# Two of q's five weight blocks as seven-product blocks, with their forms stored in DRAM by the k stage, and the split of M moved to the last stage

## The chip, the cores and the metric

One core of one Trainium2 chip. The metric is device time in microseconds (us) of one launch, the median of several runs; lower is better. One more execution is recorded by the hardware profiler, and it has a time of its own.

## The reference

`S = 2048` tokens, `D = 640`, `F = 1536`, 32 heads of 20 channels, all in f32:

```python
q, k, v = split(x @ wqkv)                       # (heads, S, 20) each
phi = lambda t: where(t > 0, t + 1, exp(t)) + 1e-6
kv  = einsum("hsd,hse->hde", phi(k), v);  z = phi(k).sum(s)
a   = (phi(q) @ kv) / (phi(q) . z + 1e-6) @ wo
b   = (sigmoid(x @ w_gate) * (x @ w_up)) @ w_down
g   = sigmoid((x * gate_w).sum(-1))
out = g * a + (1 - g) * b
```

## The kernel before

**Tiles and products.** The tokens lie in four groups of 512, taken as two pairs; pair 1 goes first, pair 0 second. Everything is transposed: weights are the stationary operand in blocks of 128 columns, the tokens of a group stream as 512 columns. For precision each f32 operand is split into a high and a low part (`split`, L219: ScalarE rounds the high part, VectorE subtracts for the low part), and each product is three passes, high·high, high·low, low·high (`mm3`, L189; its three calls are L190 to L192). "A product" in this text is one such pass.

**Stages.** The k stage (0 to 144.7 us) computes k and phi(k) for all tokens and `gt` = xᵀ·phi(k). Then come, for each pair, a q phase (`q_phase`, L1503) and an f stage (`f_phase`, L1530: gate, up and down weights, with the GLU). After the f stage of pair 0 the products of M with phi(q) end the kernel. In the q phase of pair 1 the small matrix M is made between the units: `kv_part(hg)` (L1168) multiplies a slice of `gt` with a slice of wv for six heads (the last slice has two) and keeps the block diagonal (`kvt`, then `kvh` and `kvl`), `m_part(hg)` (L1185) multiplies that with the slice of wo, and both store their results: `ms` high and low go to `mh_dram` and `ml_dram`. `m_rows` (L1317), in pair 1's f stage, reorders them into `mp_dram` with eight DRAM-to-DRAM transfers. `z_part` (L1144) follows the last unit.

**Plain units and blocks.** q's 640 columns are five blocks u of 128 columns. A plain unit `q_unit(pr, u, b, b12)` (L1011) is one block for one of the pair's two groups: five k tiles, three passes each, 15 products of 512 columns; in pair 0 two of the five tiles of group b = 1 come in halves of 256 columns. Two blocks for two groups are four units, 60 products. The f stage uses `Block` (L957) instead, which makes the four results of two weight columns times two groups in seven products of submatrices (`s1` to `s7`, a Strassen-like scheme) of 6, 9, 6, 9, 6, 9 and 9 passes, 54 in all. It needs sums of weights (`wsum`, split into `wu` of 384 columns and `ws` of 1152) and sums of tokens (`xst`, split into `xth` and `xtl`), besides the split columns themselves (`wg`). In pair 1 the weight forms are made on the spot and stored to `w_dram` (`store_w`, L793); in pair 0 they are loaded from there (`load_form`, L862). `wg` is 640 KB, `wu` 384 KB, `ws` 1152 KB, high and low parts together.

**phi.** `phi_q` (L1003) takes a product's bank through two ScalarE operations (`qe`, `qr`) and one VectorE operation into `qr`, and stores it to `p_dram` from POOL's queue. `qe` and `qr` come from a ring of four tiles.

**What sets the order.** Each engine executes its instructions in program order, and the program writes that order out by a small planner (`Order`, L47 to L158): it keeps an estimated clock for TensorE, ScalarE and VectorE; queued items (splits, sums, each with its two costs and perhaps a time from which its load is expected) are put in between the products when they fit (`_fits`: their end may be up to a slack behind TensorE's clock), or when a product needs them (`need`). `items` go ahead of `lazy`. Loads are issued by SP's queue, stores by POOL's.

Of the kernel before, what the change touches and what calls it, by code (L numbers as in the profile page):

```python
# [15 lines left out]
P = 128  # L16
# [4 lines left out]
TG = 512  # L21
# [24 lines left out]
class Order:  # L46
# [6 lines left out]
    def __init__(self):  # L53
        self.slack(False)
        self.pe = self.act = self.vec = 0.0
        self.items, self.lazy = [], []
        self.busy = False
        self.parts = self.pend = None
# [5 lines left out]
    def add(self, a, v, fn, key=None, ready=None, lazy=False, first=False):  # L64
        q = self.lazy if lazy else self.items
        q.insert(0 if first else len(q), (a, v, fn, key, ready))

    def then(self, fn):

        if self.parts is None:  # L70
            fn()
        else:
            self.parts.append(fn)

# [18 lines left out]
    def _fits(self, q):  # L93
        if not q:
            return False
        a, v, fn, key, ready = q[0]
        if ready is not None and self.pe < ready():
            return False
        end_a = self.act + a
        end = max(self.vec, end_a if a else 0.0) + v  # L100
        return not ((a and end_a > self.pe + self.slack_a) or (v and end > self.pe + self.slack_v))

    def fill(self):
        if self.busy:
            return
        while True:
            for q in (self.items, self.lazy):
                if self._fits(q):
                    self._run(q.pop(0))
                    break  # L110
            else:
                if self.pend and max(self.vec, self.pend[2]) + self.pend[3] <= self.pe + self.slack_v:
                    self._flush()
                return
# [11 lines left out]
    def need(self, key, now=True):  # L126
        for q in (self.items, self.lazy):
# [40 lines left out]
def gated_mix_kernel(ctx: ExitStack, tc: tile.TileContext, xt, xn, wk, wv, wo, wst_q, wst_f, out_t):  # L168
# [79 lines left out]
    w_dram = {}  # L248
    m_dram = [dram.tile([D, D], F32, name=n) for n in ("mh_dram", "ml_dram")]
# [143 lines left out]


# [70 lines left out]
    def queue_ks():  # L465
        for s, sums in ((1, (0, 2, 1)), (0, ()), (2, ()), (3, (3,))):
            for j in range(2):
                for t in sums:
                    order.add(0, v_cost(HW), lambda t=t, j=j: k_sum(t, j))
            for j in range(2):  # L470
                order.add(a_cost(HW), v_cost(HW), lambda s=s, j=j: k_form(s, j), ("ks", s))
        order.add(a_cost(HW), 2 * v_cost(HW), k_fifth_d, ("ks", 5))

# [254 lines left out]
    for c in range(1, 4):  # L728
        ck = chunks[c]
        if c == 1:  # L730
            a, b = KPlain(2), KPlain(3)
            order.need((ck, "plain"))
            queue_ks()
            queue_xn(2)
            for k in range(KC):
                a.k(k)
                order.fill()
            a.phi_a()
            for k in range(KC):
                b.k(k)  # L740
                order.fill()
                if k == 0:
                    a.phi_b()
                    order.add(0, 0.6, constants)
            order.need(("ks", 5))
            for t in range(2):
                k_split(tok(2, t))
        else:
            a, b = KBlock(2 * c), KBlock(2 * c + 1)
            for n in range(1, 6):  # L750
                order.need((ck, n))
                if c == 2 and n >= 3:
                    order.need(("ks", (1, 0, 2)[n - 3]))
                getattr(a, f"s{n}")()
                getattr(b, f"s{n}")()
                if n == 2:
                    queue_xn(2 * c)
# [12 lines left out]
            b.s6()  # L770
            a.phi_b()
            order.need(("pk", 2 * c - 1))
            k_split(tok(2 * c, 0))
            b.s7()
            b.sum_b()
            k_split(tok(2 * c, 1))
        if c == 3:
# [15 lines left out]
            def store_w(n, i):  # L793

                w_dram[n[2], i] = dram.tile(list(WT[n, i].shape), F32, name=f"w{n[2]}{i}")
                nc.gpsimd.dma_start(w_dram[n[2], i], f32(WT[n, i]))
# [38 lines left out]
    for u in range(4, 10):  # L835
        glast.part(u, 0, 2, tags[u], out=False)
        order.fill()
        if u == 5:
            for n in range(2):
                wg_split(("q", 1, n), w_stage[n])  # L840
    p1_tail = [lambda u=u: glast.out(u) for u in range(4, 10)]
    p1_cm.__exit__(None, None, None)
# [19 lines left out]
    def load_form(n, i):  # L862
        t = (wg_tile, wu_tile, ws_tile)[i]()
        nc.sync.dma_start(f32(t), w_dram[n[2], i])
        put(n, i, t)


    entries = [("q", 1, u) for u in (0, 2, 4)] + [("f", 1, f) for f in range(FC)]
# [20 lines left out]
    def queue_q(pr, u):  # L889
# [4 lines left out]
        def fn():  # L894
            if pr:
                wg_split(m, WST[n][:, u % 2])
                if u % 2 or u == KC - 1:
                    order.then(load_w)
# [5 lines left out]
    def queue_g(n):  # L904

        order.add(a_cost(D), v_cost(D), lambda: wg_split(n, WST[n][:, 0]), ("wg", n), lambda: W_AT.get(n, 1e9),
                  first=n[2] > 1)
# [231 lines left out]
    def z_perm():  # L1139
        zperm = f32(ws_tile())[:, 0, :D]  # L1140
# [27 lines left out]
    def kv_part(hg):  # L1168
        c0, w = hg_slice(hg)
        v = MV[hg]  # L1170
        ps = ps_tile("ch")
        for m in range(KC):
# [8 lines left out]
        order.add(0, v_cost(bdn), lambda: vec2(kvl[:w, :w], kvt[:w, :w], f32(kvh[:w, :w]), OP.subtract), ("kv", hg),  # L1181
                  first=True)
        load_mv(hg + 2)

    def m_part(hg):  # L1185
# [15 lines left out]
    load_mv(1)  # L1201
    load_mo(0)
# [6 lines left out]
    d_loads = entries[3:] + [("q", 0, u) for u in range(KC)]  # L1209
# [107 lines left out]
    def m_rows():  # L1317

        for m in range(2):
            for d in range(4):  # L1320
                nc.gpsimd.dma_start(mp_dram[d * H:(d + 1) * H, :, m],
                                    m_dram[m].rearrange("(h u d) n -> d h u n", u=KC, d=4)[d])
# [180 lines left out]
    def q_phase(pr, b12, extra):  # L1503

        units = [(u, b) for u in range(KC) for b in range(2)]
# [3 lines left out]
        for j, (u, b) in enumerate(units):  # L1509
            order.need((nx[1], "plain" if b else 2))  # L1510
            q_unit(pr, u, b, b12)
            if b and u + 2 < KC:
                queue_q(pr, u + 2)
                if not pr:
                    order.need(("wg", ("q", pr, u + 2)), False)
            elif b and not pr:
                load_form(("f", 0, u + 2 - KC), 0)
            elif b and u + 2 == KC:
                queue_g(("f", pr, 0))
                queue_s(("f", pr, 0))  # L1520
            for fn in extra.get(j, ()):
                fn()
            order.fill()
        order.slack(False)
# [5 lines left out]
    def f_phase(pr, hooks={}):  # L1530
# [4 lines left out]
        def step(f, s):  # L1535
# [14 lines left out]
            after_f(f, blk, s)  # L1550
# [18 lines left out]

        step(0, 1)  # L1570
        step(0, 2)
        for f in range(FC):
# [3 lines left out]
            if not pr and f % 2 and f > 1:  # L1576
                if f == FC - 1:
                    load_m(0)
# [54 lines left out]
    extra = {j: [] for j in range(10)}  # L1633
    extra[1] += [lambda: queue_wo(1), lambda: queue_wo(0)]
    for hg in range(NHG):
        extra[hg + 3].append(lambda hg=hg: m_part(hg))
    for hg in range(NHG):
        extra[hg + 1].append(lambda hg=hg: kv_part(hg))
    extra[7].append(z_perm)
    extra[9] += [z_part, m_close]  # L1640
    q_phase(1, lambda k: [(b12h[:, k], b12l[:, k])], extra)
# [12 lines left out]
    def load_forms(f, *forms):  # L1654
        for i in forms:
            load_form(("f", 0, f), i)

    tail = f_phase(1, {
        (3, 7): [m_rows],
        (6, 7): [lambda: other[0].load()],  # L1660
        (FC - 2, 7): [lambda: load_forms(0, 1, 2)],
        (FC - 1, 2): [lambda: queue_a(0, 2), lambda: queue_a(2, 4)],
        (FC - 1, 6): [lambda: queue_a(4, 5, 2)],
        (FC - 1, 7): [lambda: load_forms(1, 1, 2), queue_b],
# [6 lines left out]
    nx[0].queue_sums()  # L1671
    nx[1].queue_sums()
# [3 lines left out]
    q_phase(0, lambda k: [(c_h[c][:, k], c_l[c][:, k]) for c in range(2)], {  # L1676
# [92 lines left out]
    tail = f_phase(0, {  # L1769
# [83 lines left out]
```

## Time and profile before

| | us |
|---|---|
| runs | 754.95, 755.49, 755.50 |
| median | 755.49 |
| profiled execution | 755.98 |
| its span in the trace | 754.3 |
| TensorE busy | 747.2 (99%) |
| VectorE busy | 547.4 (73%) |
| ScalarE busy | 308.6 (41%) |
| GpSimd (POOL) busy | 89.1 (12%) |
| q phase of pair 1 | 144.69 to 191.28 |
| f stage of pair 1 | to 421.89 |
| q phase of pair 0 | 421.89 to 456.37 |

A row of the timeline has the start, the duration, engine, line, operation, output and inputs, shape, and in brackets how long the engine was idle before it and what ended that. Matmuls overlap, so the distance between their starts, not their duration, is what each costs. A row of a window has the stretch, its length, the busy time of TensorE, weight loads, VectorE, ScalarE and GpSimd with the instruction counts, the granted clock of TensorE, the DMA share and GB/s. A row of TensorE's waits has who waited for whom, the total in us, how often, and the longest. A row of a group has the count, then busy us and mean ns, then the idle time ahead of it and what ended it. A row of DMA issues has the count, KB each and median us from issue to landing.

### The profile page before, as it was taken

How to read it: one execution, taken by the hardware profiler on the slowest of the kernel's cores; microseconds unless marked ns; L12 is line 12 of the kernel's file. 1: busy time of each engine (PE TensorE's matmuls, PEld its weight loads, DVE VectorE, ACT ScalarE, POOL GpSimd, SP SyncE). 2: the span in 40 equal slices, each digit the busy share in tenths (PEclk: the TensorE clock that was granted, in tenths of full speed). 3: DMA queues.
4: the chain of work that ended last, by engine and by line, in shares of the span. 5: the costliest groups of instructions: out<-in, count | busy, mean ns of one | idle time of the engine just before them, and what ended most of it. 6: DMA issues, size and time to landing. Idle time of an engine off the chain costs nothing.

```text
span 754.3 us, 10042 instructions
## 1 busy us (share of the span) xinstructions
PE 747.2 (99%) x3696; PEld 641.1 (85%) x3696; DVE 547.4 (73%) x963; ACT 308.6 (41%) x578; POOL 89.1 (12%) x146
## 2 busy tenths in 40 slices
PE   9999999999999999999999999999999999999998
PEld 7999999988888888888888888888888888887886
DVE  4877575887676678877788864575868776886864
ACT  5664537266555534343344444253323223212110
POOL 0210111023222322112121210000000000000000
PEclk9999999999999999999999999999999999999999
DMA  8553537787887797776475744965454546277333
GB/s 260 122 160 71 140 63 185 191 275 247 312 316 271 262 386 286 266 271 226 181 261 221 297 164 154 356 244 206 158 227 150 225 137 244 91 267 254 114 134 117
DMA packets 60518, 160.51 MB, mean 213 GB/s; under 512 B 9575, under 2 KB 23399, under 8 KB 57269
## 3 DMA queue, kind: packets, MB, share of 16 engines
q1 hardware_dynamic: 44933, 99.15, 39.3%
q0 software_dynamic: 15392, 60.56, 22.9%
q8 instruction: 29, 0.48, 0.3%
q14 instruction: 20, 0.16, 0.1%
q10 hardware_dynamic: 144, 0.16, 0.1%
HBM read 97.33 MB, written 60.56 MB: 209 GB/s over the span
## 4 chain that ended last, share of the span: by engine, by line
PE 80%; DMA 3%; DVE 1%; ACT 1%; SPq 0%; issue 0%
PE dd L190 8%; PE dd L192 8%; PE dd L191 8%; PE ch L190 7%; PE ch L191 7%; PE ch L192 7%; PE rot L191 6%; PE rot L190 6%; PE rot L192 6%; PE cc L190 5%; PE cc L191 5%; PE cc L192 5%; DMA pden<-p_dram 2%; DMA wv_sb<-wv 1%; PE ch L1173 1%; DMA xnst<-xn 1%
## 5 line engine op out<-in xcount | busy, mean ns | idle before, releaser
L202 ACT ACTIVATE c<-ch 128x512 f32<-128x512 f32 x72 | 43.0, 597 | 161.7 <-PE ch L192 159.9
L206 DVE TENSOR_TENSOR hf<-c,hf 128x512 fp32r<-128x512 f32 x63 | 43.2, 688 | 28.0 <-ACT hf L202 27.7
L206 DVE TENSOR_TENSOR tb<-dd,tb 128x512 f32<-128x512 f32 x75 | 51.1, 688 | 14.2 <-PE dd L192 13.9
L206 DVE TENSOR_TENSOR c<-cc,c 128x512 f32<-128x512 f32 x48 | 32.9, 685 | 30.3 <-ACT c L202 23.4
L202 ACT ACTIVATE c<-c 128x512 f32<-128x512 f32 x48 | 30.2, 628 | 49.7 <-DVE c L206 49.7
L206 DVE TENSOR_TENSOR tb<-rot,tb 128x512 f32<-128x512 f32 x64 | 43.5, 687 | 6.0 <-PE rot L192 5.7
L202 ACT ACTIVATE hf<-c 128x512 fp32r<-128x512 f32 x63 | 39.3, 625 | 18.2 <-DVE c L206 17.3
L190 PE MATMUL dd<-xrh,wg 128*128 128x512 f32 x102 | 40.0, 392 | 0.0
L192 PE MATMUL dd<-xrh,wg 128*128 128x512 f32 x102 | 39.8, 390 | 0.0
L191 PE MATMUL dd<-xrl,wg 128*128 128x512 f32 x102 | 39.8, 390 | 0.0
L190 PE MATMUL ch<-xth,ws 128*128 128x512 f32 x96 | 37.3, 389 | 0.0
L191 PE MATMUL ch<-xtl,ws 128*128 128x512 f32 x96 | 37.3, 389 | 0.0
L192 PE MATMUL ch<-xth,ws 128*128 128x512 f32 x96 | 37.3, 389 | 0.0
L191 PE MATMUL rot<-pkl,xnh 128*128 128x320 f32 x102 | 31.7, 311 | 1.0 <-DVE pkl L210 0.6
L190 PE MATMUL rot<-pkh,xnh 128*128 128x320 f32 x102 | 31.5, 309 | 0.0
L192 PE MATMUL rot<-pkh,xnl 128*128 128x320 f32 x102 | 31.4, 308 | 0.0
L206 DVE TENSOR_TENSOR c<-c,c 128x512 f32<-128x512 f32 x44 | 30.2, 686 | 1.3 <-ACT c L202 0.9
L190 PE MATMUL cc<-xbh,ws 128*128 128x512 f32 x72 | 28.0, 389 | 0.0
L191 PE MATMUL cc<-xbl,ws 128*128 128x512 f32 x72 | 28.0, 389 | 0.0
L192 PE MATMUL cc<-xbh,ws 128*128 128x512 f32 x72 | 28.0, 389 | 0.0
L202 ACT ACTIVATE pq<-pl 128x512 fp32r<-128x512 f32 x14 | 8.5, 631 | 39.0 <-DVE pl L210 39.0
L1103 POOL DMA_DIRECT2D om_dram<-om x4 | 2.2, 540 | 186.9 <-ACT om L202 186.9
(473 smaller groups left out, 2309.3 us busy)
## 6 DMA issues: line engine op xcount, KB each, us to landing
w<-ws POOLq DMA_DIRECT2D x12, 1152.0 KB, 6.6
ws<-w SPq DMA_DIRECT2D x12, 1152.0 KB, 7.8
wst<-wst_f SPq DMA_DIRECT2D x12, 640.0 KB, 4.8
w<-wg POOLq DMA_DIRECT2D x12, 640.0 KB, 5.0
wd<-wd POOLq DMA_DIRECT2D x12, 640.0 KB, 6.5
wg<-w SPq DMA_DIRECT2D x12, 640.0 KB, 4.1
xst<-xt SPq DMA_DIRECT2D x10, 640.0 KB, 7.0
wf<-wd SPq DMA_DIRECT2D x10, 640.0 KB, 5.7
```

The lines of the kernel that those rows point to most:

```text
L190: nc.tensor.matmul(out, l_hi, r_hi, start=first, stop=False, skip_group_check=True)
L191: nc.tensor.matmul(out, l_hi, r_lo, start=False, stop=False, skip_group_check=True)
L192: nc.tensor.matmul(out, l_lo, r_hi, start=False, stop=last, skip_group_check=True)
L202: nc.scalar.activation(out, src, fn, **kw)
L206: nc.vector.tensor_tensor(out, a, b, op=op)
L1103: nc.gpsimd.dma_start(om_dram[:, g], om)
L1173: nc.tensor.matmul(ps[:w, :w], v[:, m, :w], gt[:, m, c0:c0 + w], start=(m == 0), stop=(m == KC - 1))
```

## The change

- q's blocks u = 2 and 3 go through `Block(("q", pr, 2))` in both pairs; blocks 0, 1 and 4 stay plain units (`Q_PLAIN`). In pair 1 the block's products s1 to s7 follow the last units; kv parts and M parts stand between them, the last ones on the bank pair `rot`. In pair 0 `q_phase` is a generator whose last products s5 to s7 alternate with the first products of the f stage's first block, whose sigmoid is held until after its s3.
- The weight forms of blocks 2 and 3 are made in the k stage by a new `queue_qw(2)`, as lazy items: one load, ten splits, five sums and ten stores to `w_dram["q", 2, i]`; both q phases load them back.
- `m_part` stores M in f32 as it is (`m_dram`), `m_rows` reorders it with four transfers into `mr_dram`, and a new `queue_m` loads it in five pieces in the f stage of pair 0, splits each and stores it to `mp_dram`. These are in a new queue `spare`, behind `lazy`.
- The wv slices have three buffers instead of two. `z_perm` uses a tile of pool `m1`.
- `Order` has queues `urgent` (any item of it that fits may go), `spare` and `soon`: `follow` puts a VectorE step (phi's last, `kvl`) off until the clock of VectorE has come to the point where ScalarE is done.
- In pair 0 `queue_both` takes the sums and splits of both halves of the tokens in turns.
- The f stage's first forms in pair 1 are queued earlier in the q phase (`queue_s` after block 1, `queue_g` after block 4).

```diff
+    def queue_qw(u):
+        raw = qs.tile([P, 2, D], F32, name="qraw", tag="qraw")
+        nc.sync.dma_start(raw, wst_q[:, u:u + 2])
+        at = max(order.pe, order.vec) + 5.0
...
+            def fn():
+                t = qs.tile([P, 2, w], F32R, name="qp", tag="qp", bufs=3)
+                split(t[:, 0, :n], t[:, 1, :n], src)
+                order.then(lambda: nc.gpsimd.dma_start(w_dram["q", u, i][:, :, c:c + n], f32(t[:, :, :n])))
...
-    def phi_q(g, u, src):
+    def phi_q(g, u, src, after="p"):
         e, r = tt("qe"), tt("qr")
-        act(e, src, AF.Exp, "p")
+        act(e, src, AF.Exp, after)
         act(r, src, AF.Relu)
-        vec3(r, e, 1.0, r, OP.min, OP.add, "a")
-        nc.gpsimd.dma_start(p_dram[:, u, g], r)
+        def rest():
+            vec3(r, e, 1.0, r, OP.min, OP.add)
+            nc.gpsimd.dma_start(p_dram[:, u, g], r)
+        order.need("phi")
+        order.follow(v_cost(TG), rest, "phi")
...
-            v = mp.tile([P, KC, bdn], F32, name="wv_sb", tag="wv_sb", bufs=2)
+            v = mp.tile([P, KC, bdn], F32, name="wv_sb", tag="wv_sb", bufs=3)
...
-        ms = [m1_tile(t, "ms", F32R, bdn) for t in ("ma", "mb")]
+        ms = m1_tile(("ma", "mb")[hg % 2], "ms", F32, bdn)
         for h in range(2):
-            ps = ps_tile("cc")
+            ps = ps_tile(tag)
             cs = slice(h * HALF, (h + 1) * HALF)
             mm3(ps[:w, :HALF], kvh[:w, :w], kvl[:w, :w], woh[:w, cs], wol[:w, cs], True, True)
-            split(ms[0][:w, cs], ms[1][:w, cs], ps[:w, :HALF], "p")
-        for m, dst in zip(ms, m_dram):
-            nc.gpsimd.dma_start(dst[c0:c0 + w], f32(m[:w]))
+            act(ms[:w, cs], ps[:w, :HALF], AF.Copy, "p")
+        nc.gpsimd.dma_start(m_dram[c0:c0 + w], ms[:w])
...
+    def queue_m(u=0):
+        raw = down_pool[1].tile([P, D], F32, name="mr", tag="mr")
+        nc.sync.dma_start(raw, mr_dram[:, u])
...
+            t = down_pool[1].tile([P, 2, D], F32R, name="mt", tag="mt")
+            split(t[:, 0], t[:, 1], raw)
+            def rest():
+                nc.gpsimd.dma_start(mp_dram[:, u], f32(t))
+                if u + 1 < KC:
+                    queue_m(u + 1)
+            order.then(rest)
+        order.add(a_cost(D), v_cost(D), fn, "m", lambda: at, spare=True)
...
     def q_phase(pr, b12, extra):
-        units = [(u, b) for u in range(KC) for b in range(2)]
+        units = [(u, b) for u in Q_PLAIN for b in range(2)]
+        n = ("q", pr, 2)
...
+        blk = Block(n)
+        for s in range(1, 8):
+            if s > 1:
+                order.need((nx[0] if pr else nx[1], s if s < 7 else 2))
+            getattr(blk, f"s{s}")()
+            if s == 3:
+                phi_q(2 * pr, 2, blk.c11, "v")
+            elif s == 6:
+                phi_q(2 * pr + 1, 3, blk.c22, "v")
+                phi_q(2 * pr, 3, blk.ch)
+            elif s == 7 and pr:
+                phi_q(2 * pr + 1, 2, blk.c12, "v")
...
+            for fn in extra.get(j + s, ()):
+                fn()
+            order.fill()
+            if not pr and s > 4:
+                yield
```

More of the change, by code (lines that the diff above doesn't have):

```diff
@@ L73, in then, with follow, follow_up @@
             self.parts.append(fn)
+    def follow(self, v, fn, key=None):
+        self.soon.append((self.act, v, fn, key))
+    def follow_up(self, n=1):
+        for at, v, fn, key in self.soon[:n]:
+            self.soon.pop(0)
+            was, self.busy = self.busy, True
+            self.vec = max(self.vec, at)
+            fn()
+            self.busy = was
     def _flush(self):
@@ L247, in gated_mix_kernel @@
     om_dram = dram.tile([P, NG, TG], F32, name="om_dram")
-    w_dram = {}
-    m_dram = [dram.tile([D, D], F32, name=n) for n in ("mh_dram", "ml_dram")]
+    m_dram = dram.tile([D, D], F32, name="m_dram")
+    mr_dram = dram.tile([P, KC, D], F32, name="mr_dram")
     bdn = HPG * DH
@@ L392, in queue_forms, with queue_both @@
         nx[0].queue_sums()
+    def queue_both(nx):
+        w = 2 * CW
+        for n, t, k in ((0, 1, 3), (0, 0, 4), (0, 2, 5), (3, 3, 6)):
+            for c in nx:
+                for m in {(0, 1): (0, 1, 2), (3, 3): (3,)}.get((n, t), ()):
+                    order.add(0, v_cost(w), lambda c=c, m=m: c.sum(m), None, lambda c=c: c.at)
+            for c in nx:
+                order.add(a_cost(w), v_cost(w), lambda c=c, t=t: c.form(t), (nx[1], k) if c is nx[1] else None)
     pa_cm = tc.tile_pool(name="pa", bufs=1, side="right")
@@ L840, in gated_mix_kernel @@
                 wg_split(("q", 1, n), w_stage[n])
+    order.need("qw")
     p1_tail = [lambda u=u: glast.out(u) for u in range(4, 10)]
+    qs_cm.__exit__(None, None, None)
     p1_cm.__exit__(None, None, None)
@@ L863, in load_form @@
         t = (wg_tile, wu_tile, ws_tile)[i]()
[L864 removed]
+        nc.sync.dma_start(f32(t), w_dram[n[::2] + (i,)])
         put(n, i, t)
[L868 removed]
+    Q_PLAIN = (0, 1, 4)
+    entries = [("q", 1, u) for u in (0, 4)] + [("f", 1, f) for f in range(FC)]
     WST, WS, W_AT = {}, {}, {}
@@ L1180, in kv_part, with m_part @@
         KV[hg] = (kvh, kvl)
[L1181 to L1185, printed above, removed]
+        order.follow(v_cost(bdn), lambda: vec2(kvl[:w, :w], kvt[:w, :w], f32(kvh[:w, :w]), OP.subtract), ("kv", hg))
+        load_mv(hg + 3)
+    def m_part(hg, tag="cc"):
         c0, w = hg_slice(hg)
@@ L1201, in gated_mix_kernel @@
     load_mv(1)
+    load_mv(2)
     load_mo(0)
@@ L1208, in gated_mix_kernel @@
     wd_dram = {}
-    d_loads = entries[3:] + [("q", 0, u) for u in range(KC)]
+    d_loads = entries[2:] + [("q", 0, u) for u in Q_PLAIN]
     tb = None
@@ L1317, in m_rows, with fn @@
     def m_rows():
[L1319 to L1322, printed above, removed]
+        for d in range(4):
+            nc.gpsimd.dma_start(mr_dram[d * H:(d + 1) * H], m_dram.rearrange("(h u d) n -> d h u n", u=KC, d=4)[d])
+    def queue_m(u=0):
+        raw = down_pool[1].tile([P, D], F32, name="mr", tag="mr")
+        nc.sync.dma_start(raw, mr_dram[:, u])
+        at = max(order.pe, order.vec) + 9.0
+        def fn():
+            t = down_pool[1].tile([P, 2, D], F32R, name="mt", tag="mt")
[6 more added lines that the diff above has]
+        order.add(a_cost(D), v_cost(D), fn, "m", lambda: at, spare=True)
     def m_close():
@@ L1511, in q_phase @@
             q_unit(pr, u, b, b12)
[L1512 to L1520, printed above, removed]
+            if b:
+                if u == 0:
+                    queue_q(pr, 4)
+                    if not pr:
+                        order.need(("wg", ("q", pr, 4)), False)
+                elif u == 1:
+                    load_form(n, 0)
+                    if pr:
+                        queue_s(("f", pr, 0))
+                elif pr:
+                    load_form(n, 1)
+                    load_w()
+                    queue_g(("f", pr, 0))
+                else:
+                    load_form(("f", 0, 0), 0)
+            elif pr and u == 4:
+                load_form(n, 2)
             for fn in extra.get(j, ()):
@@ L1549, in step @@
                 tails[f - 1][s]()
-            after_f(f, blk, s)
+            if s == 3 and f == 0 and not pr:
+                for _ in q:
+                    pass
+                after_f(f, blk, 2)
+            elif s != 2 or f or pr:
+                after_f(f, blk, s)
             if s == 7:
@@ L1577, in f_phase @@
                 if f == FC - 1:
+                    while any(it[3] == "m" for it in order.spare) or order.pend:
+                        order.need("m")
+                        order._flush()
                     load_m(0)
@@ L1632, in gated_mix_kernel @@
         fn()
-    extra = {j: [] for j in range(10)}
+    extra = {j: [] for j in range(13)}
     extra[1] += [lambda: queue_wo(1), lambda: queue_wo(0)]
[L1635 to L1641, printed above, removed]
+    for hg, j in enumerate((3, 4, 5, 7, 8, 10)):
+        extra[j].append(lambda hg=hg, t="cc" if j < 8 else "rot": m_part(hg, t))
+    for hg, j in enumerate((1, 2, 3, 4, 5, 6)):
+        extra[j].append(lambda hg=hg, t="ch" if j < 6 else "rot": kv_part(hg, t))
+    extra[6].insert(0, lambda: order.need(("wo", 3), False))
+    extra[8].insert(0, lambda: order.need(("wo", 4), False))
+    extra[10].append(z_perm)
+    extra[12] += [z_part, m_close]
+    q = q_phase(1, lambda k: [(b12h[:, k], b12l[:, k])], extra)
     def queue_a(k0, k1, key=None):
```

113 lines of the change are left out of this document (82 added, 31 removed).

## The prediction

> **What bounds the kernel now.** I read the page first, then the waits of TensorE, the busy time by window, the groups of the first q phase by form and the timeline around its one wait.
>
> ```profile
> PE 747.2 (99%) x3696; PEld 641.1 (85%) x3696; DVE 547.4 (73%) x963; ACT 308.6 (41%) x578; POOL 89.1 (12%) x146
> PE 80%; DMA 3%; DVE 1%; ACT 1%; SPq 0%; issue 0%
> PE rot L282 <- DVE warm L279: 1.3, 1, 1.3
> PE rot L191 <- DVE pkl L210: 0.6, 1, 0.6
> PE rot L191 <- DVE pq L206: 0.4, 1, 0.4
> PE ch L1173 <- DMA wv_sb<-wv: 0.2, 1, 0.2
> 144.69:191.28 46.59, 46.37 (x248) 38.77 (x247) 38.11 (x75) 28.61 (x59) 12.19 (x22) 1.00 0.86 267
> 421.89:456.37 34.48, 34.48 (x182) 29.71 (x181) 25.41 (x40) 16.59 (x30) 5.77 (x11) 1.00 0.53 182
> 456.40:650.00 193.60, 193.43 (x854) 159.61 (x852) 134.69 (x223) 65.68 (x115) 2.16 (x4) 1.00 0.58 210
> 60.00:80.00 20.00, 20.00 (x138) 20.00 (x137) 13.63 (x24) 9.64 (x19) 1.19 (x1) 1.00 0.27 66
> 160.00:180.00 20.00, 19.78 (x118) 16.92 (x117) 15.09 (x31) 12.77 (x28) 5.17 (x10) 1.00 0.98 317
> ```
>
> TensorE is busy 99% at a granted clock of 1.00, and its waits sum to about 3 us. So a product taken out shortens the span unless something new stalls TensorE. The windows (us, then busy us of PE, weight load, DVE, ACT, POOL, then clock, DMA share, GB/s) show where: the first q phase (144.69 to 191.28) has VectorE at 38.11 of 46.59 us and DMA at 0.86, in 160 to 180 at 0.98. The second (421.89 to 456.37) is easier, the k stage (60 to 80) and the second f stage have room. The first phase decides.
>
> **Products removed.** A block of two weight columns over two groups takes 54 products in place of 60. The changed program has the same 2,556 products of 512 columns and 66 in place of 90 of 256: pair 1 goes from 60 of 512 to 54; pair 0 from 48 of 512 and 24 of 256 to 54 of 512.
>
> ```profile
> 147.22 0.39 PE L192 MATMUL dd<-xah,wg 128*128 128x512 f32 x1
> 149.94 0.39 PE L192 MATMUL dd<-xrh,wg 128*128 128x512 f32 x1
> 427.33 0.28 PE L190 MATMUL rot<-b12h,wg 128*128 128x256 f32 x1
> 428.76 0.40 PE L190 MATMUL dd<-xrh,wg 128*128 128x512 f32 x1
> ```
>
> There are 12 starts between the first two rows and 12 between the last two: 0.227 and 0.119 us each. Pair 1 saves 6×0.227 = 1.36; pair 0 saves 24×0.119 − 6×0.227 = 1.50; together **2.86 us**. The Trainium skill, "TensorE: Matmul & The Clock Gate", section "Back-to-back issue gap", gives about 131 ns per product of 512 in a sustained stream and 216 for an isolated one; by 131 the six would be worth 0.8, and the whole change 0.6 less. The trace differs from the sustained figure and is close to the isolated one, so the measurement stands.
>
> **The wait that goes.** With three buffers for wv instead of two, kv_part(3) need not wait for its load.
>
> ```profile
> 160.54 0.32 PE L190 MATMUL cc<-woh,kvh 120*120 120x320 f32 x1
> 161.43 1.21 PE L1173 MATMUL ch<-gt,wv_sb 128*120 128x120 f32 x10
> 162.41 0.48 PE L190 MATMUL dd<-xrh,wg 128*128 128x512 f32 x1
> 166.68 0.31 PE L192 MATMUL cc<-woh,kvl 120*120 120x320 f32 x1
> 167.21 1.31 PE L1173 MATMUL ch<-gt,wv_sb 128*120 128x120 f32 x10 [0.22 <-DMA wv_sb<-wv]
> ```
>
> An M part takes 161.43 − 160.54 = 0.89, so 0.15 a product; from the last product of the next one, 167.21 − 166.68 = 0.53, 0.38 too long. The row calls 0.22 of it waiting. I take **0.35** as gain.
>
> **New stall 1, the product s3 of pair 1.** The order on TensorE is as before until the unit at 162.41. Then come, by the rows above: unit 3.41 (15×0.227), M part 0.89, kv part 0.98, unit 3.41, M part 0.89, kv 0.98, s1 1.36, the narrow kv 0.4 (estimate), s2 2.04, M part 0.89: s3 is due at 162.41 + 15.25 = 177.7. It adds to a bank that ScalarE must first copy out; ScalarE's copy stands behind kvh of kv part 4, that behind VectorE's kvt. So the question is when VectorE gets there. Its order in the changed program, behind qr at 161.96, has a sum on a reloaded xst at once; before, that sum stood four instructions on and ran at 166.15.
>
> ```profile
> 161.96 0.69 DVE L210 SCALAR_TENSOR_TENSOR qr<-qe,qr 128x512 f32<-128x512 f32 x1 [0.69 <-ACT qr L202]
> 166.15 1.41 DVE L206 TENSOR_TENSOR xst<-xst 128x512 f32<-128x512 f32 x2
> L325 SPq DMA_DIRECT2D xst<-xt x2: 463/464/466, 159.0 to 159.5; - x2
> DMA to landing us min/median/max: 5.2/5.7/6.1
> L206 DVE TENSOR_TENSOR xst<-xst 128x512 f32<-128x512 f32 x8 | 5.5, 685 | 0.1
> L206 DVE TENSOR_TENSOR xtl<-xst,xth 128x512 fp32r<-128x512 f32 x8 | 5.3, 687 | 1.6 <-ACT xth L202 1.6
> L206 DVE TENSOR_TENSOR wol<-wo_sb,woh 120x640 fp32r<-120x640 f32 x5 | 4.1, 820 | 0.8 <-ACT woh L202 0.7
> L206 DVE TENSOR_TENSOR wsum<-wst 128x256 f32<-128x256 f32 x2 | 0.8, 416 | 0.0
> L206 DVE TENSOR_TENSOR kvl<-kvt,kvh 120x120 fp32r<-120x120 f32 x5 | 1.4, 282 | 1.5 <-ACT kvh L202 1.5
> L202 ACT ACTIVATE c<-ch 128x512 f32<-128x512 f32 x72 | 43.0, 597 | 161.7 <-PE ch L192 159.9
> L206 DVE TENSOR_TENSOR ms<-cc,ms 120x320 fp32r<-120x320 f32 x10 | 4.4, 482 | 0.0
> ```
>
> The part issued last of the two (159.5) lands up to 6.1 us later, 165.6, so VectorE stands idle for three microseconds that it used before. Behind that sum it has, each at the mean less the 0.08 by which neighbours overlap: 4 sums 2.4, 4 xtl 2.4, 2 wol 1.5, 2 qr 1.2, 4 kvt or kvl 0.8, 5 wsum 1.7 (the full width taken for all), 1 wg 0.74 (as a wol): 10.7. Its waits for ScalarE by the rows (1.6/8 four times, 0.8/5 and 1.5/5 twice) add 1.7. That gives 178.0; kvt, kvh and the copy (0.597) end a microsecond later, near 178.9. Stall: **1.2 us**. Bounds: nothing, if the load lands at the lower end and the waits overlap; 2.5, if the queue (0.98 busy) makes the load two more microseconds late, of which the chain hands on most.
>
> **New stall 2, s3 of f0.** M parts no longer need their lows on VectorE, but phi's tiles qe and qr come from a ring of four. The block's last qr reuses the tile of c22, whose store to p_dram stands in POOL's queue behind f0's form of 1152 KB.
>
> ```profile
> w<-ws POOLq DMA_DIRECT2D x12, 1152.0 KB, 6.6
> p_dram<-qr POOLq DMA_DIRECT2D x20, 256.0 KB, 3.0
> mp_dram<-ml_dram POOLq DMA_DIRECT2D x4, 400.0 KB, 9.9
> 191.29 1.17 PE L1149 MATMUL ch<-ones_f,ws 128*128 128x1 f32 x10
> 192.32 0.48 PE L190 MATMUL ch<-xah,wg 128*128 128x512 f32 x1
> ```
>
> From s3 at 178.9, products s3, M part, s4 and s5 take 1.36 + 0.89 + 2.04 + 1.36, and a copy and an add of 0.6 each evacuate c22 by 185.8; the form's store is issued at about that time (its lows stand just ahead of that add), and c22's own after phi, at 187.2. It lands at 185.8 + 6.6 = 192.4, the p store about 0.9 behind it (estimate from 256 KB at the 267 to 317 GB/s of the windows): 193.3. Then qr 0.6, a small logit operation 0.2 and ScalarE's copy of f0's bank 0.6: 194.7. TensorE is due at f0's s3 at 178.9 + 39 products 8.84 + two M parts 1.78 + the z products 1.03 + s1 and s2 of f0 3.40, with 0.3 for two small steps (estimate): 194.25. Stall: **0.45**. Bounds: nothing, if the store lands 0.5 earlier; 3.8, in the second rival. The Trainium skill, "DMA: Bandwidth & Descriptors", section "Anatomy of one DMA — SWDGE (gpsimd) path", fits 2.0 us + bytes/436e3, so 4.7 us for this form; by that the store is 1.9 earlier and the sum would keep this 0.45. The row's 6.6 is larger, and it decides.
>
> **Loads and stores on the path.** The 1152 KB form for the q block is issued near 167.8; with the bytes queued ahead at 317 GB/s it lands at 177 (estimate), 2 us before s3. Nothing is added for it; late, it costs what it is late. The other forms are needed later than that.
>
> **K stage.** queue_qw adds 10 splits, 5 sums and 10 stores. At the 0.416 of 256 columns the 15 VectorE steps take up to 6 us, the ScalarE steps as much at most (0.597 for 512 columns), spread over some 50 us in which VectorE has 6 of every 20 idle (row 60 to 80). They are queued behind all other work. The only waits of TensorE there are those for pkl (0.6, near the stage's end), whose chain begins with a load that does not move. Cost 0; if a split stands ahead of phi and the chain is as tight as at pkl, 0.6 once, up to 1.5 if two or three add up.
>
> **Pair 0.** Its q phase leaves 9 us of VectorE idle and DMA at 0.53; forms are loaded ahead, the sum there is zero. M's lows leave the first phase and come back in the second f stage: 5 splits of 128x640, 5×0.74 on VectorE, with 59 of 193.6 us idle there, and one load and one store each. Cost 0; if a piece stands ahead of an evacuation, at most its 0.74 each. The 0.4 for pq stays.
>
> **Sum.** −2.86 − 0.35 + 1.2 + 0.45 = −1.56. The profiled execution took 755.98, 1.7 more than its span of 754.3, and 0.49 above the median; from it the sum gives 754.4, from the median 755.49 it gives **753.9**. A difference under 0.2% (1.5 us) is what a measurement of this kernel can't tell from no change.
>
> **Rivals.**
>
> *All hidden.* The reload lands before VectorE asks, and neither stall comes: 755.49 − 3.21 = 752.3; with half a microsecond left of the stalls, 752.8. For it: VectorE loses the lows of M, 4.4 us by their row, for three more adds of a block (3×0.61). Against it: the order puts the sum ahead of its load by four instructions of the old order, and the lows that go do not shorten what stands between the load and kvt 4. Chance 0.28.
>
> *Slower: the ring of phi's tiles.* POOL's transfers are the slow ones where they meet loads: a store of only 400 KB took 9.9 us (row). If c22's store takes that, it lands at 187.2 + 9.9 = 197.1; f0's copy ends at 198.5 in place of 194.7, TensorE waits 3.8 more than forecast: 757.7. Slower than before begins with c22's store later than 193.3 + 1.6 = 194.9; slower by 0.2% at 196.4. Against it: the same store's median is 3.0. Chance 0.18.
>
> *The forms late, or the k stage felt.* If the q block's form lands 2 us behind need (180.9), or phi is delayed once by 1.5 in the k stage, the result is 755.4 to 755.9. For it: DMA 0.98. Chance 0.12.
>
> That the change does not do what it says is ruled out for the products, which the order of the program shows gone.
>
> **How the numbers follow.** The forecast, 753.9 with its own range of 752.9 to 755.2 (each stall between half and twice), has 0.42; 0.28 of that is below 754.0 (faster by over 0.2%), 0.14 within. All hidden adds 0.28 to faster. The ring gives 0.16 slower and 0.02 within; late forms 0.10 within and 0.02 slower. Faster 0.56, same 0.26, slower 0.18. The range runs from 752.1 (all hidden, less the measurement's scatter) to 756.8, which leaves out most of the slower rival.
>
> **What would show it.** Right: 24 fewer products of 256; no wait for wv; a wait of about 1.2 us ahead of pair 1's s3 with VectorE idle for xst before it, and one of about half a microsecond ahead of f0's s3. Wrong: no such waits (all hidden); a wait of several microseconds at f0's s3 (the ring); a wait of s3 on the load of ws (late forms); new waits for pkl at 60 to 100 us (k stage); or a product of the new block at another spacing than 0.227.

## The result and the profile after

The changed kernel takes **753.97 us** in the median of 18 runs (752.55 to 757.20), the kernel before 755.45 (18 runs, 753.85 to 757.01): ratio **0.9982, interval 0.9975 to 0.9989**, 1.4 us at the median of before. The forecast was 753.9. Two later comparisons of the same kernel gave 0.9989 (0.9980 to 0.9998) and 0.9994 (0.9984 to 1.0004), 0.8 and 0.5 us: the gain lies between half a microsecond and the 1.4 of the first comparison, so the forecast of 1.56 stands at its upper end.

The lines of the page and of TensorE's waits that answer to those of before:

```profile
span 750.8 us, 10048 instructions
PE 744.7 (99%) x3672; PEld 638.5 (85%) x3672; DVE 551.6 (73%) x973; ACT 315.6 (42%) x595; POOL 94.1 (13%) x151
PE 93%; DVE 3%; DMA 2%; ACT 1%; issue 0%; SPq 0%
PE rot L308 <- DVE warm L305: 1.3, 1, 1.3
PE rot L217 <- DVE pkl L236: 0.4, 1, 0.4
PE rot L217 <- DVE pq L232: 0.4, 1, 0.4
PE ch L216 <- ACT c L228: 0.4, 1, 0.4
```

The 24 products are gone (3,672 in place of 3,696), the wait for wv too, and one wait is new: ch for ScalarE's copy, 0.4. This execution is 3.5 us shorter than the traced one of before, more than twice what the medians say, so one pair of traces is not enough. The window of the first q phase up to f0's first product, before and after (the kernel before runs 1.04 us longer here than in the row shown ahead, which stops at the z products), and 33.0 us from the second q phase's first product in the changed kernel:

```profile
144.69:192.32 47.63, 47.41 (x259) 39.80 (x257) 38.42 (x75) 29.40 (x61) 12.75 (x23) 1.00 0.86 268
143.97:190.45 46.48, 46.12 (x252) 38.44 (x251) 33.31 (x64) 28.25 (x59) 9.15 (x17) 1.00 0.92 310
420.04:453.04 33.00, 33.00 (x164) 27.97 (x163) 26.50 (x47) 17.05 (x31) 4.78 (x9) 1.00 0.58 204
```

VectorE has 33.3 us of work in the first phase in place of 38.4, and DMA is busier there, 0.92 in place of 0.86. TensorE is never idle in the stretch of the second.

Since traces of one kernel differ, I give each trace's length by stage, from starts of TensorE's products in the timelines: the k stage up to the first product with wg; the first q phase up to f0's first product; then 235.0 us up to the first product of 256 columns (235.01 to 235.05 in all traces but one, told below); the second q phase and f stage up to the first product of the last stage; the last stage to the end of TensorE's work.

| trace | k stage | first q phase | second half | last stage |
|---|---|---|---|---|
| before | 144.69 | 47.63 | 254.17 | 69.12 |
| before_again | 143.92 | 47.16 | 253.81 | 69.13 |
| m_alone | 145.46 | 47.33 | 254.15 | 69.16 |
| forms_alone | 144.09 | 47.27 | 254.59 | 69.75 |
| arrays_only | 144.78 | 46.99 | 254.42 | 69.59 |
| the changed kernel | 143.97 | 46.48 | 252.15 | 69.63 |
| after_again | 145.16 | 46.18 | 252.51 | 69.76 |
| after_third | 144.36 | 45.94 | 253.71 | 69.88 |
| pair1_only | 144.79 | 46.94 | 253.91 | 69.73 |
| omg_first | 145.49 | 46.43 | 253.33 | 69.13 |
| xst_late | 143.90 | 49.23 | 252.39 | 69.32 |
| both_fixes | 144.81 | 46.95 | 252.85 | 69.12 |
| three_fixes | 143.85 | 49.09 | 252.14 | 69.13 |
| two_fixes | 144.41 | 47.06 | 252.14 | 69.12 |

### The profile page after: what moved, and what is told of

It reads as the page before. It is cut to its first block, busy times and chain, and to the rows that moved or that the text cites. A ratio compares the mean times of both kernels' runs of the same rounds, so it can differ in the third digit from the quotient of the medians.

```text
span 750.8 us, 10048 instructions
## 1 busy us (share of the span) xinstructions
PE 744.7 (99%) x3672; PEld 638.5 (85%) x3672; DVE 551.6 (73%) x973; ACT 315.6 (42%) x595; POOL 94.1 (13%) x151
## 4 chain that ended last, share of the span: by engine, by line
PE 93%; DVE 3%; DMA 2%; ACT 1%; issue 0%; SPq 0%
PE ch L216 9%; PE ch L217 9%; PE ch L218 9%; PE dd L216 9%; PE dd L217 9%; PE dd L218 9%; PE rot L217 7%; PE rot L218 7%; PE rot L216 7%; PE cc L217 6%; PE cc L216 6%; PE cc L218 6%; DMA omg<-om_dram 1%; DVE tb L232 1%; PE ch L1263 1%; DMA xnst<-xn 1%
## 5 line engine op out<-in xcount | busy, mean ns | idle before, releaser
L228 ACT ACTIVATE c<-ch 128x512 f32<-128x512 f32 x78 | 46.6, 597 | 166.4 <-PE ch L218 164.6
L232 DVE TENSOR_TENSOR c<-cc,c 128x512 f32<-128x512 f32 x52 | 35.7, 686 | 26.7 <-ACT c L228 20.0
L216 PE MATMUL ch<-xth,ws 128*128 128x512 f32 x104 | 40.6, 390 | 0.4 <-ACT c L228 0.4
L217 PE MATMUL ch<-xtl,ws 128*128 128x512 f32 x104 | 40.5, 389 | 0.0
L218 PE MATMUL ch<-xth,ws 128*128 128x512 f32 x104 | 40.5, 389 | 0.0
L216 PE MATMUL dd<-xrh,wg 128*128 128x512 f32 x96 | 37.6, 392 | 0.0
L217 PE MATMUL dd<-xrl,wg 128*128 128x512 f32 x96 | 37.4, 390 | 0.0
L218 PE MATMUL dd<-xrh,wg 128*128 128x512 f32 x96 | 37.4, 390 | 0.0
L218 PE MATMUL cc<-xbh,ws 128*128 128x512 f32 x78 | 30.3, 389 | 0.0
L216 PE MATMUL cc<-xbh,ws 128*128 128x512 f32 x78 | 30.3, 389 | 0.0
L217 PE MATMUL cc<-xbl,ws 128*128 128x512 f32 x78 | 30.3, 389 | 0.0
L216 PEld LDWEIGHTS ch<-xth,ws 128*128 128x128 f32 x104 | 19.5, 188 | 4.7 <-ACT c L228 0.6
```

The costliest lines, as they stand in the source:

```text
L216: nc.tensor.matmul(out, l_hi, r_hi, start=first, stop=False, skip_group_check=True)
L217: nc.tensor.matmul(out, l_hi, r_lo, start=False, stop=False, skip_group_check=True)
L218: nc.tensor.matmul(out, l_lo, r_hi, start=False, stop=last, skip_group_check=True)
L228: nc.scalar.activation(out, src, fn, **kw)
L232: nc.vector.tensor_tensor(out, a, b, op=op)
```

## Experiments: is the trace typical, and what is each part worth

**after_again, before_again: both kernels unaltered.**

> The changed kernel itself, unaltered, for a second trace and more times. Its first traced execution was 3.4 us below the traced one of the kernel before, while the medians differ by 1.5. Theory S (executions differ): the waits of the first q phase (pair 1's s3, f0's s3) and of the k stage are decided by when transfers land, so this trace shows other waits than the first (s3 0.2 to 1.5 us, f0's s3 0 to 1 us), a span between 750.8 and 753, and a median near 754.0. Theory L (the trace is typical and the medians are not): the span is again within 0.4 us of 750.8 and the median near 752.5.

> The kernel before, unaltered, for a second trace. Theory S: the span differs from 754.3 by up to 1 us, in the waits for transfers (pkl near 121 us, wv near 167, pden near 490) and not in the spacing of products; ratio 1.000 within 0.001. Theory L: span within 0.3 us of 754.3.

Theory S holds, and the traces of the kernel before differ even more than it allowed, by 1.6 us. after_again: span 752.2, median 754.23 (11 runs). before_again: span 752.7, median 755.05 (11 runs), ratio 0.9996 (0.9987 to 1.0004). Executions differ by more than a microsecond, most of it in the k stage (143.85 to 145.49 over all kernels, with no order by kernel), which the change does not shorten. s3's loss against the usual spacing of products was 0.52 in the first trace and 0.29 here, and no trace shows a wait at f0's s3.

**m_alone: M's split moved by itself.** Edit: `m_part`, `m_rows`, `queue_m` and the queue `spare` of the change put into the kernel before, and with them a compiler option that the changed kernel also sets, `dynamic_dma_scratch_size=8192`.

> The kernel before with only M's split moved: M stored in f32 by m_part, four reordering transfers instead of eight, five pieces split in pair 0's f stage; the scratch for transfers at 8192 as in the changed kernel. Products as before. Theory of the prediction: cost zero, span and median within 0.4 us of the kernel before, no new wait of TensorE between 490 and 680 us, VectorE 4.4 us less busy in the first q phase. Rival: pieces stand ahead of evacuations, up to 0.7 us each, 0.7 to 3 us slower.

Median 755.13 (11 runs), ratio 0.9987 (0.9978 to 0.9996), span 754.5, all stages as before: no cost, as forecast. But ws of the block needed near 533 us landed 11.1 us after its issue, where the four traces without M's pieces have 7.9 to 8.3. It cost nothing here; it does below.

**pair1_only: pair 0's block back to plain units.** Edit: `units = [(u, b) for u in (Q_PLAIN if pr else range(KC)) for b in range(2)]`, with the loads of before in pair 0.

> The changed kernel with all five of pair 0's blocks as plain units again; pair 1's block, the forms of the k stage and M's move stay. It has 6 products of 512 less than the kernel before. Theory of the prediction: pair 0's block is worth 1.5 us with no stall, so this is 1.5 us above the changed kernel, about 755.4, and its trace shows the s3 wait of pair 1 and no wait in the second q phase. Rival: pair 0's block costs something in the second q phase that its trace hid, so this is 0 to 0.7 above the changed kernel.

755.72 (11 runs) against 754.23 for the changed kernel in the same comparison: pair 0's block is worth 1.5 us in the medians, as its products say (1.1 by the ratios to the kernel before, and the runs don't settle it finer). Its second half, 253.91, is that of the kernel before. Against the kernel before the ratio is 1.0004 (0.9995 to 1.0013): pair 1's block with all that it needs gains nothing that these runs can show. In this trace its 1.36 us of products meets 0.92 us of waits in the first q phase and 0.6 in the last stage.

**forms_alone, arrays_only: the forms made but not read; their arrays alone.** Edits to the kernel before (cut to their main lines; forms_alone also has the scratch of 8192, arrays_only does not):

```diff
+                    queue_qw(2)                                   # forms_alone
...
+                    for i, n in enumerate((D, 3 * P, 9 * P)):     # arrays_only
+                        w_dram["q", 2, i] = dram.tile([P, 2, n], F32, name=f"wq2{i}")
...
+    for i in range(3):
+        nc.gpsimd.dma_start(w_dram["q", 2, i][:, 0, :P], ones_f)
```

> The kernel before with queue_qw(2) added: the forms of blocks 2 and 3 are made and stored in the k stage, and nobody reads them; the scratch for transfers is at 8192. Products as before. Prediction: cost zero; span and median within 0.5 us of the kernel before; the k stage (first product of q) starts between 143.9 and 145.5 as in the traces so far. Rival on the k stage: one or two new waits for pkl between 60 and 110 us, 0.6 to 1.5 us slower. On the last stage, where every trace with the new blocks took 69.6 to 69.8 us and every trace without 69.1 to 69.2: if the stored forms are the reason, because p_dram and om_dram come to lie elsewhere in DRAM behind nine more arrays, this run has the last stage at 69.6 and its lone load of om near 737 us takes 4.2 to 4.5 us; if the q phases are, 69.1 and 3.0 to 3.4.

> The kernel before with nothing of the forms but their three arrays in DRAM (640, 384 and 1152 KB), each written once by a small store near the end of the k stage. Theory A (it is where the arrays lie: the three arrays move p_dram and om_dram to other addresses, or something about them): the lone load of om near 737 us takes 4.2 to 4.5 us, VectorE waits about 8.4 us for om near 724, the last stage takes 69.6 to 69.8 us. Theory B (it is the scratch size of 8192 together with the forms' work in the k stage): 3.0 to 3.4 us, 7.3 us and 69.1.

(The arrays are three, not nine as the first text says, 2176 KB together.) forms_alone: 755.93 (12 runs), ratio 1.0006 (0.9997 to 1.0015); its k stage, 144.09, is among the shorter ones, so making the forms costs nothing there. But its last stage took 69.75, though nothing in it was touched, and arrays_only (a single run, 756.22) has much the same, 69.59, while m_alone, which has the scratch of 8192 and no arrays, has 69.16. Theory A holds in so far as three more arrays in DRAM suffice. VectorE's wait for om in before, before_again, forms_alone and arrays_only:

```profile
724.41 3.10 DVE L206 TENSOR_TENSOR tb<-tb,omg 128x512 f32<-128x512 f32 x5 [7.24 <-DMA omg<-om_dram]
722.90 3.10 DVE L206 TENSOR_TENSOR tb<-tb,omg 128x512 f32<-128x512 f32 x5 [7.34 <-DMA omg<-om_dram]
725.12 2.50 DVE L206 TENSOR_TENSOR tb<-tb,omg 128x512 f32<-128x512 f32 x4 [8.49 <-DMA omg<-om_dram]
725.22 1.90 DVE L206 TENSOR_TENSOR tb<-tb,omg 128x512 f32<-128x512 f32 x3 [8.34 <-DMA omg<-om_dram]
```

The load takes 5.3 and 5.4 us in the first two and 6.5 and 6.4 in the others. The next load of om, with no other load beside it, shows it plainest (times to landing of before, then of arrays_only):

```profile
L1720 SPq DMA_DIRECT2D omg<-om_dram x1: 457/457/457, 736.9 to 736.9; - x1
DMA to landing us min/median/max: 3.4/3.4/3.4
...
L1724 SPq DMA_DIRECT2D omg<-om_dram x1: 448/448/448, 737.7 to 737.7; - x1
DMA to landing us min/median/max: 4.3/4.3/4.3
```

What it is about the arrays (their addresses, or what shares a memory bank with them) no run tells.

## Experiments: taking the waits away

**omg_first.** Edit in the last stage, at `gi == 1`: `load_b(groups[2])` ahead of `load_p(groups[3])`.

> The changed kernel with the load of om (and b) for the third group of the last stage issued ahead of three loads of p, instead of behind them. Theory (the last stage lost half a microsecond because VectorE waits 8.4 us for om, whose load took 6.4 to 6.5 us instead of 5.3, and its splits of pq then come late for the product at 732): VectorE's multiplication with om starts about 3 us earlier after the load's issue, the wait of TensorE near 732 goes, the last stage takes 69.1 us instead of 69.7, median about 753.6. Rival (the load is not on the path): the last stage stays at 69.6 to 69.8.

The last stage is 69.13. In the changed kernel's first trace a product at 732.05 starts 0.23 us late; that is gone, and so it is in all four traces with this edit. VectorE's row for om, the changed kernel and then this one:

```profile
721.69 3.10 DVE L232 TENSOR_TENSOR tb<-tb,omg 128x512 f32<-128x512 f32 x5 [8.39 <-DMA omg<-om_dram]
720.49 3.10 DVE L232 TENSOR_TENSOR tb<-tb,omg 128x512 f32<-128x512 f32 x5 [4.53 <-DMA omg<-om_dram]
```

Median 753.45 (10 runs), ratio 0.9972 (0.9960 to 0.9984). Its trace had another wait, of TensorE for a form of pair 0's f stage:

```profile
533.34 0.47 PE L216 MATMUL ch<-xth,ws 128*128 128x512 f32 x1 [0.67 <-DMA ws<-wf]
```

M's pieces are issued just ahead of that form (the load of the third, 320 KB, at 519.89, the store of the second, 640 KB, at 520.16, ws at 520.47), in a stretch with three loads of down weights; ws took 12.7 us.

**xst_late, both_fixes.** Edit: `nx[0].at = order.pe + 7.5` behind the reload of xst; both_fixes has omg_first's too.

> The changed kernel with the time at which the planner expects the reloaded xst set 7.5 us after its issue instead of 4; the sums of tokens come later in VectorE's order, kvt 4 ahead of three steps on weights. Theory of the prediction (VectorE's wait for xst is what makes pair 1's s3 late): VectorE's wait for xst falls from 2.6 us to 1 us or less, and the wait at s3 (0.3 to 0.5 us in three traces) goes; the first q phase takes about 46.0 us instead of 46.2 to 46.5; median 0.3 below the changed kernel's. Rival (s3 waits for the load of ws or for ScalarE itself): s3's wait stays at 0.3 to 0.5.

> Both of the other two edits: om loaded first in the last stage, and xst expected later. If both theories hold, neither the wait at s3 nor the one near 732 is there, the first q phase takes 46.0 and the last stage 69.1 us, together 0.9 us below the changed kernel: about 753.2 in the median. If neither: 754.1.

A miss that teaches. VectorE's wait for xst falls from 2.64 to 1.57 and the one at s3 is gone, but in xst_late the first q phase took 49.23, and in both_fixes, where that wait was 0.96, 46.95: the planner put the halves of wo and kvt elsewhere, and other products waited. So the edit does not test the wait at s3 by itself. The products that waited in xst_late:

```profile
171.76 0.41 PE L216 MATMUL cc<-woh,kvh 120*120 120x320 f32 x1 [1.11 <-ACT ms L228]
174.37 0.50 PE L216 MATMUL ch<-xah,wg 128*128 128x512 f32 x1 [0.42 <-DVE kvt L232]
181.49 0.41 PE L216 MATMUL rot<-woh,kvh 120*120 120x320 f32 x1 [0.43 <-ACT woh L228]
182.35 0.41 PE L217 MATMUL rot<-wol,kvh 120*120 120x320 f32 x1 [0.45 <-DVE wol L232]
```

Medians 755.02 (ratio 0.9993, 0.9984 to 1.0003) and 754.48 (0.9988, 0.9975 to 1.0002), 12 runs each.

**three_fixes, after_third, two_fixes.** three_fixes queues f0's sums (`queue_s(("f", 1, 0))`) behind kv part 5, has om first, and begins M's pieces at `(2, 4)` instead of `(2, 7)`; two_fixes leaves the sums where the change has them.

> The changed kernel with three edits: om loaded ahead of p in the last stage; the sums of f0's weights queued behind kv part 5, so that VectorE's kvt 4 stands ahead of five sums; M's pieces begun in the fourth product of the third block of pair 0's f stage instead of the seventh, which takes the second piece out of the queue ahead of the form ws that came late near 532 us. If each stage's wait is what the traces say: first q phase 45.9 to 46.1 us without a wait at s3 (46.2 to 46.5 in the changed kernel), no wait for ws near 532 (0 to 0.8 us before), last stage 69.1; the median 1 to 1.4 us below the changed kernel, 752.6 to 753.2. Rival for the first q phase: the wait moves to f0's s3, because its forms are made later, 0.3 to 1 us; then only the last stage and 532 gain, 753.4.

> The changed kernel itself for a third trace, and for times on the same chip as the three edits. By its first two traces: k stage 143.9 to 145.5, first q phase 46.2 to 46.5 with 0.3 to 0.5 at s3, second half 252.1 to 253.3 with 0 to 0.8 for ws near 532, last stage 69.6 to 69.8; median 753.9 to 754.4.

> The changed kernel with om loaded ahead of p in the last stage, and M's pieces begun in the fourth product of the third block of pair 0's f stage; the sums of f0's weights stay where the changed kernel has them. By stages: first q phase 45.9 to 46.5 us as in the changed kernel, its ring wait of ScalarE 0.7 to 1.6 us with no wait of TensorE at f0's s1; from the second q phase to the last stage 252.1 to 252.5, without a wait for ws near 532 (four traces with the pieces at their old place had 0, 0.26, 0.83 and 1.47 there); last stage 69.1. Median about 1 us below the changed kernel's 754.2, 753.2. Rival (the wait near 532 comes from the loads of that block alone, not from M's piece ahead of it): again a wait of up to 1.5 us there in some runs, median 753.6.

after_third: 754.77 (12 runs), above what was expected; no wait at s3 this time, but the longest for ws:

```profile
532.13 0.47 PE L216 MATMUL ch<-xth,ws 128*128 128x512 f32 x1 [1.31 <-DMA ws<-wf]
```

What TensorE lost there goes with the time that ws took: 11.8, 12.0, 12.2, 12.5, 12.7 and 13.4 us to landing in the six traces with both blocks and M's pieces at their old place, and 0, 0.13, 0.26, 0.59, 0.83 and 1.47 us lost. With the pieces begun earlier, no piece stands between that form's loads, ws took 11.4 and 10.4, and the two traces lost nothing: both second halves are 252.14, where the six give 252.15 to 253.71. Two traces, and one of the six lost nothing either, so the traces make the worth of this edit likely and do not settle it. Part of the lengthening has another cause, for 10.4 is still above 8.1; which one stays open.

three_fixes: 755.05 (12 runs), ratio 0.9997 (0.9985 to 1.0010). The sums, the one edit that two_fixes lacks, cost more than they free. VectorE waited 3.07 for xst, and 1.58 us were lost at an M part. The rival is there too, at f0's first product instead of s3. ScalarE, TensorE and two windows around:

```profile
192.30 0.60 ACT L228 ACTIVATE qr<-ch 128x512 f32<-128x512 f32 x1 [3.04 <-DMA p_dram<-qr]
192.95 0.59 PE L216 MATMUL ch<-xah,wg 128*128 128x512 f32 x1 [1.32 <-ACT qr L228]
193.33 0.63 PE L217 MATMUL ch<-xal,wg 128*128 128x512 f32 x1
193.76 0.63 PE L218 MATMUL ch<-xah,wg 128*128 128x512 f32 x1
190.00:193.00 3.00, 1.68 (x14) 1.51 (x12) 0.07 (x1) 0.60 (x1) 0.00 (x0) 1.00 1.07 424
193.00:196.00 3.00, 3.00 (x8) 2.36 (x9) 1.62 (x4) 1.54 (x4) 0.54 (x1) 0.54 0.90 312
```

ScalarE's qr waited for a store of phi (the ring), TensorE could not have the bank, and then the clock fell (last section).

two_fixes: **753.08** (5 runs, 752.22 to 753.23), ratio **0.9960 (0.9946 to 0.9973)**, 3.0 us below the kernel before by the ratio and 2.4 by the medians: faster than the kernel before, and by this ratio than the changed kernel, which was not in the same comparison. omg_first's interval overlaps with this one, so the times do not show what M's pieces add to om. The first q phase, 47.06, was longer than expected, with 0.51 us lost at an M part and 0.54 at s3.

## Why the prediction was right, and where it was not

The total was right because its misses cancel, which is luck: the two stalls were 1.4 us too large, and about as much that the sum did not have stood in their place (the last stage, M's pieces, the k stage, a smaller gain at wv). Means by stage, three traces of the changed kernel against two of before: k stage +0.19, first q phase 47.40 to 46.20, −1.20; second half 253.99 to 252.79, −1.20; last stage 69.13 to 69.76, +0.63; together −1.6. The forecast had 0, −0.06 (−1.36 − 0.35 + 1.65), −1.50 and 0.

**Products removed: right.** 24 fewer, at the same spacing; pair 0's 1.5 came out by itself in pair1_only, within its noise. One remark beside the sum was wrong: at another price for a product of 512 columns the whole change would not be worth 0.6 less. It has as many of these as before, so their price drops out, and the 2.86 is 24×0.119.

**The wait that goes: oversized.** It is 0.38 and 0.23 us in two of the five traces that still have two wv buffers, and nothing in three; 0.35 was one execution's.

**Stall 1, s3 of pair 1: right chain, oversized.** In the changed kernel VectorE, then TensorE:

```profile
164.52 0.69 DVE L232 TENSOR_TENSOR xst<-xst 128x512 f32<-128x512 f32 x1 [2.64 <-DMA xst<-xt]
176.88 0.28 DVE L232 TENSOR_TENSOR kvt<-ch,bd 120x120 f32<-120x120 f32 x1
178.03 0.50 PE L216 MATMUL ch<-xth,ws 128*128 128x512 f32 x1 [0.36 <-ACT c L228]
```

The idle three microseconds came (2.64), and kvt 4 stood 32.9 us after the phase's start (forecast 178.0 − 144.69 = 33.3). The mis-sized term is when s3 was due: half a microsecond later than I had it. The sum took 0.227 for every product, but where the shape changes the second product starts only 0.31 to 0.34 after the first. So the stall was 0.52, 0.29 and nothing in three traces in place of 1.2. It was not the load of ws: that had landed 3.5 us before s3. What sets the loss is when xst lands. In the six traces with the same order (after_third, after_again, the first trace, omg_first, pair1_only, two_fixes) the sum on it started 20.07, 20.33, 20.55, 20.58, 21.07 and 21.19 us after the phase's start, and the phase lost 0, 0.29, 0.52, 0.55, 0.92 and 1.05 at s3 and the M part ahead of it: nearly one for one.

**Stall 2: right mechanism, wrong tile.** ScalarE does wait for a store of phi, but for the tile of c11, whose store stands ahead of the 1152 KB form, and with qr of the bank ch, not of c12:

```profile
189.79 0.60 ACT L228 ACTIVATE qr<-ch 128x512 f32<-128x512 f32 x1 [1.61 <-DMA p_dram<-qr]
192.97 0.58 ACT L228 ACTIVATE c<-ch 128x512 f32<-128x512 f32 x1
```

(c11's store was issued at 184.06, the form's at 185.46.) f0's copy ends at 193.6, and f0's s3 started at 193.97 without a wait: the 0.45 was nothing. The cover is thin, 0.4 us here; three_fixes shows the price of a longer wait on the ring, and so what the slower rival stood for.

**M's pieces: the step that failed.** "Cost 0" counted VectorE's 0.74 as the price and named load and store without placing them in the queue. They lengthen the load of a form behind them (8.1 to 11.1 us in m_alone), and in the changed kernel, where it took 11.8 to 13.4, that came to 0, 0.26 and 1.47 us of TensorE's time in three traces. It is hidden in the mean of the second half, because a loss near 490 us went, which the forecast did not have: a product there started late by 0.10 to 0.89 us in all six traces without pair 0's block (0.46 and 0.10 in the two of before) and not at all in the three traces of the changed kernel. Why it went, no run tells.

**Not in the forecast: the last stage,** +0.2 to 0.75 in each of the seven traces with the arrays and om behind p. No step of the prediction looked at loads whose arrays and neighbours the change leaves alone.

**K stage and loads of the block: right.** They cost nothing; ws of the block landed 7.5 us after its issue at 167.0, 3.5 us before s3.

## What to carry to other kernels

Where TensorE is 99% busy, products taken out are worth their spacing; the question is only which hidden chain they lay bare, and each of them must be looked for in the DMA queues as well as on the engines: what is queued right ahead of a load with little time to spare. A prediction of a microsecond needs more than one trace, for a wait of 0.4 us in one execution is 0 or 1.5 in the next. A load on which an engine waits goes ahead of those it does not yet need, and other traffic out of its way: with two such reorderings the gain was about twice that of the change alone.

## What the hardware showed that I had not expected

With three more arrays in DRAM, in arrays_only hardly written and never read, a lone 256 KB load of another array takes 4.0 to 4.5 us (seven traces with om behind p) in place of 3.0 to 3.4 (three traces without the arrays). In the four traces with om ahead of p, the arrays there too, the same load takes 3.7 to 3.9. It is not the chip: before_again and m_alone ran on the same one as after_again and pair1_only.

In the trace of three_fixes TensorE had only ten products of one column and then a wait between 190.46 and 192.95, and the granted clock was 0.54 from 193 to 196: products of 512 columns started 0.427 us apart in place of 0.227, 1.6 us more than the wait itself. It is not this execution alone: over the whole execution the granted clock is 0.997 or 0.998 in seven of the twelve runs, which took 755.04 to 757.62 us, and 0.999 or 1.000 in the five others, 753.27 to 754.38. Losses of 1.5 and 1.6 us behind full products (near 532 in after_third, near 172 in three_fixes) left the clock at 1.00. The Trainium skill, "TensorE: Matmul & The Clock Gate", section "HAM oscillation — how this bites in real kernels", warns of idle gaps over about 3.4 us; here 2.5 us with little work in them went ahead of the drop, in the one trace that shows it.
